# One decode step of attention plus feed-forward: half a weight tile on eight of the sixteen DMA engines

## The chip, the cores and the metric

The kernel runs on one core of a Trainium2 chip. The core has five engines with a queue each (TensorE, which the profile calls PE; VectorE, DVE; ScalarE, ACT; GpSimd, POOL; SyncE, SP) and sixteen DMA engines that bring data from HBM into SBUF (128 partitions). Matrix products end in PSUM. The metric is the device time of one execution in microseconds (us), the median of several; lower is better.

## The reference

One token for each of two batch rows. With `xn = layernorm(x)` (D = 1024):

```python
q = xn @ wq                                  # 32 heads of 128
p = softmax(q @ k.T * 128**-0.5)             # 4 key/value heads, 32768 cached keys each
attn = (p @ v) @ wo
h = silu(xn @ w1)                            # F = 3584
out = x + attn + h @ w2
```

All of it is float32. The caches of keys and values and the four weight matrices are read once, 331 MB in all; the arithmetic on them is small, since only two tokens are computed.

## The kernel before

**Tiling and staging.** Three buffers of 128 x 16384 floats (8 MB each), `bufA`, `bufB` and `bufC`, take everything that is streamed. First `wq` and `w1` come in: the projections give the queries (`qall`) and `pre`, the input of silu, and from it `hT` (L213 to L217), which holds `h` transposed: row tile f of the 3584 hidden values (28 tiles of 128) as 128 partitions x 2 tokens, spread over 32 columns. Then a loop of eight turns, one for each key/value head and batch row, loads two halves of the keys and two halves of the values. The two output projections come last: `wo` (32 row tiles of 128 x 1024) in bufA and bufC, then `w2` (28 row tiles) in bufB (16 tiles) and in bufA (12 tiles).

**What sets the order.** The order is written out by hand; each engine runs its own instructions in program order and waits on semaphores. SP issues all loads in one queue (`load`, L204 to L208), each after the TensorE work that frees its buffer. A load of 128 partitions is split over all sixteen DMA engines, and its semaphore has risen by 16 when all of them are done.

**The tail.** The last 12 row tiles of `w2` come in nine pieces (`stream`, L334 to L341, called at L378), cut smaller towards the end: 6 tiles, 2 tiles, 1, 1, 1, and the last tile in quarters. TensorE (`tiles`, L351) waits for the piece that holds a row tile (L353) and multiplies it. Row tiles are numbered through `wo` and `w2`: t = 0 to 31 is wo, 32 to 59 is w2. Up to t = 55 a tile is two matmuls of 512 columns, which go to two of the four 32-column strips of the array (`acc2`). From t = 56 on, a tile is four matmuls of 256 columns, j = 0 to 3, one for each strip of `acc` (L371). Ahead of t = 58 four `fold` matmuls add what `acc2` holds, which DVE has summed with x into `ob` (L363). The last tile, t = 59, is four groups of four matmuls of 64 columns, a group for each quarter. ACT then copies `acc` to SBUF and issues the store of the output (L388, L389).

The instructions of interest have helper lines in the profile: L98 is every matmul, L208 every load of SP after the first three, L52 a semaphore that the instruction stream counts down.

## Time and profile before

| | us |
|---|---|
| median of 3 runs | 774.31 |
| lowest and highest | 773.94 and 774.92 |
| the profiled execution, its own time | 773.65 |
| its span, first to last instruction | 772.2 |
| TensorE busy | 386.6 (50%) |
| VectorE busy | 120.7 (16%) |
| ScalarE busy | 27.3 (4%) |
| DMA, mean over the span | 429 GB/s |

The span is what the trace covers; some 1.5 us of the execution's own time lie around it. The profiled execution was a little shorter than the three runs. A share of DMA is the mean over the sixteen DMA engines, so 0.50 may be eight engines that are busy and eight that have nothing left. "Idle before" is the time that an engine stood still ahead of a group, with what ended it.

### The profile page before, as it was taken

How to read it: one execution, taken by the hardware profiler on the slowest of the kernel's cores; microseconds unless marked ns; L12 is line 12 of the kernel's file. 1: busy time of each engine (PE TensorE's matmuls, PEld its weight loads, DVE VectorE, ACT ScalarE, POOL GpSimd, SP SyncE). 2: the span in 40 equal slices, each digit the busy share in tenths (PEclk: the TensorE clock that was granted, in tenths of full speed). 3: DMA queues.
4: the chain of work that ended last, by engine and by line, in shares of the span. 5: the costliest groups of instructions: out<-in, count | busy, mean ns of one | idle time of the engine just before them, and what ended most of it. 6: DMA issues, size and time to landing. Idle time of an engine off the chain costs nothing. (4 is left out here: it accounts for less than half of the span.)

```text
span 772.2 us, 5903 instructions
## 1 busy us (share of the span) xinstructions
PE 386.6 (50%) x2736; PEld 122.7 (16%) x2736; DVE 120.7 (16%) x153; ACT 27.3 (4%) x33; POOL 3.0 (0%) x10
## 2 busy tenths in 40 slices
PE   1545645554545444645454545444645454545466
PEld 1111211111111111211111111111211111111112
DVE  2000013111311131113111311131113111311000
ACT  0000101000100010001000000010001000000000
POOL 1000000000000000000000000000000000000000
PEclk9977677677677677677677677677677677677679
DMA  9999999999999999999999999999999999999997
GB/s 384 435 435 435 431 435 435 435 435 435 435 435 435 435 435 431 431 435 435 435 431 431 435 435 435 435 435 435 435 435 435 435 431 435 435 435 435 421 417 321
DMA packets 7091, 331.48 MB, mean 429 GB/s; under 512 B 798, under 2 KB 1318, under 8 KB 1708
## 3 DMA queue, kind: packets, MB, share of 16 engines
q1 hardware_dynamic: 7056, 331.35, 99.4%
q8 instruction: 6, 0.10, 0.0%
q10 hardware_dynamic: 28, 0.02, 0.0%
q14 instruction: 1, 0.01, 0.0%
HBM read 331.37 MB, written 0.01 MB: 429 GB/s over the span
## 5 line engine op out<-in xcount | busy, mean ns | idle before, releaser
L98 PE MATMUL ps<-bufB,qT 128*32 128x512 f32 x512 | 72.7, 731 | 83.2 <-PEq L52 83.2
L98 PE MATMUL po<-bufB,st 128*32 128x512 f32 x512 | 71.5, 721 | 82.7 <-PEq L52 82.7
L98 PE MATMUL ps<-bufA,qT 128*32 128x512 f32 x512 | 71.7, 723 | 53.1 <-PEq L52 53.1
L98 PE MATMUL po<-bufA,st 128*32 128x512 f32 x512 | 72.2, 727 | 39.3 <-PEq L52 39.3
L276 DVE TENSOR_REDUCE ls<-st 128x8 f32<-128x1024 f32 x16 | 31.8, 1984 | 229.6 <-PE po L98 229.6
L251 DVE STREAM_TRANSPOSE st<-ps 128x1024 f32<-128x1024 f32 x16 | 20.0, 1250 | 250.6 <-PE ps L98 250.6
L98 PEld LDWEIGHTS ps<-bufB,qT 128*32 128x32 f32 x512 | 20.0, 131 | 136.0 <-issue 136.0
L98 PEld LDWEIGHTS po<-bufB,st 128*32 128x32 f32 x512 | 19.7, 130 | 134.5 <-issue 134.5
L98 PEld LDWEIGHTS ps<-bufA,qT 128*32 128x32 f32 x512 | 19.8, 130 | 98.4 <-issue 98.4
L98 PEld LDWEIGHTS po<-bufA,st 128*32 128x32 f32 x512 | 19.9, 131 | 85.0 <-issue 85.0
L253 DVE TENSOR_REDUCE mx<-st 128x8 f32<-128x1024 f32 x16 | 31.7, 1981 | 0.6
L273 ACT ACTIVATE st<-st 128x1024 f32<-128x1024 f32 x16 | 16.9, 1056 | 358.7 <-DVE st L272 358.0
L98 PE MATMUL ps<-bufB,xnT 128*32 128x512 f32 x112 | 18.3, 730 | 14.8 <-PEq L52 14.8
L272 DVE TENSOR_TENSOR st<-st,gmax 128x1024 f32<-128x1024 f32 x16 | 18.9, 1222 | 0.3
L98 PE MATMUL smA<-ident,rm 128*8 128x128 f32 x16 | 3.7, 317 | 29.5 <-PEq L52 29.5
L98 PE MATMUL ps<-bufC,xnT 128*32 128x512 f32 x64 | 8.6, 698 | 10.8 <-DMA bufC<-in_w 10.8
L98 PE MATMUL ps<-bufC,oT 128*32 128x512 f32 x64 | 8.5, 692 | 9.7 <-DMA bufC<-in_wo 9.7
L281 ACT COPY ob<-po 128x512 f32<-128x512 f32 x8 | 4.7, 585 | 236.7 <-PE po L98 236.7
L98 PE MATMUL smA<-lsum,ones 128*128 128x8 f32 x16 | 3.3, 278 | 19.2 <-PEq L52 19.2
L98 PE MATMUL ps<-bufA,oT 128*32 128x512 f32 x64 | 9.6, 766 | 6.6 <-DMA bufA<-in_wo 6.6
L98 PE MATMUL ps<-bufA,xnT 128*32 128x512 f32 x64 | 9.7, 773 | 5.0 <-PEq L52 5.0
L98 PE MATMUL ps<-bufB,hT 128*32 128x512 f32 x64 | 8.9, 702 | 4.8 <-DMA bufB<-in_w 4.8
(65 smaller groups left out, 102.1 us busy)
## 6 DMA issues: line engine op xcount, KB each, us to landing
bufB<-in_w SPq DMA_DIRECT2D x1, 6144.0 KB, 26.2
bufB<-in_w SPq DMA_DIRECT2D x1, 5632.0 KB, 42.7
bufA<-in_w SPq DMA_DIRECT2D x1, 3072.0 KB, 36.3
bufB<-in_w SPq DMA_DIRECT2D x1, 2560.0 KB, 48.5
bufA<-in_w SPq DMA_DIRECT2D x3, 512.0 KB, 40.0
bufA<-in_w SPq DMA_DIRECT2D x1, 1024.0 KB, 38.4
bufA<-in_w SPq DMA_DIRECT2D x4, 128.0 KB, 38.0
bufA<-in_kt SPq DMA_DIRECT2D x8, 29.3
```

Source lines behind the costliest of these rows:

```text
L98: return nc.tensor.matmul(o, lhsT, rhs, start=start, stop=stop)
L251: t = dve.mark(V.transpose(st[:, 2 * c:2 * c + 2].rearrange("p a j m -> p (a j m)"), pair[c]))
L253: m = V.tensor_reduce(mx[:, c, :], st[:, 2 * c:2 * c + 2].rearrange("p a j (r m) -> p m (a j r)", r=4), AX.X, ALU.max)
L272: act.wait(dve.mark(V.tensor_sub(e8[c], e8[c], gmax.to_broadcast([P, 128, REP]))))
L273: nc.scalar.activation(e8[c], e8[c], AF.Exp, scale=SCALE).then_inc(te, 1)
L276: m = V.tensor_reduce(ls[:, c, :], e8[c].rearrange("p n m -> p m n"), AX.X, ALU.add)
L281: nc.scalar.copy(ob, po).then_inc(tob, 1)
```

## The change

It concerns row tile 25 of `w2` (`LOW = FT - 3`, t = 57), the third last. Before, it came as one piece of 128 partitions x 1024 columns. Now its columns 0 to 511 come as a piece of 128 partitions x 512 columns. Its columns 512 to 1023, all 128 rows, go to partitions 0 to 63 of an unused part of bufA: rows 0 to 63 lie in the first 512 columns there, rows 64 to 127 behind them. One transfer with a semaphore of its own (`low`) does that, with the source's outermost dimension of size 8, each index covering eight neighbouring partitions.

Since rows 64 to 127 now stand on partitions 0 to 63, the values of `h` that they meet must stand there too. So one further matmul transposes them to partitions 0 to 63, a copy puts them into an added 29th column of `pre`, and silu runs over 29 columns instead of 28. In the output projection strips j = 2 and j = 3 of t = 57 take two matmuls each over 64 partitions, instead of one over 128. That tile waits for `low` and its own piece.

```diff
-    oT, hT = sb("oT", P, HQ, 32), sb("hT", P, FT, 32)
-    pre, sig, rsig = (sb(n, P, FT, B) for n in ("pre", "sig", "rsig"))
+    oT, hT = sb("oT", P, HQ, 32), sb("hT", P, FT + 1, 32)
+    pre, sig, rsig = (sb(n, P, FT + 1, B) for n in ("pre", "sig", "rsig"))
...
+        if u == 3:
+            j, i = divmod(LOW - 16, 4)
+            xo = ps[2 + u % 2][:, 8 * parts:8 * parts + B]
+            m = mm(xo, pr[u % 2][:n, i * P + 64:i * P + 192], ident[:n, 32 * j:32 * j + B])
...
+            if u == 3:
+                m = V.tensor_copy(pre[:, FT, :], xo)
...
+            if t == HQ + LOW:
+                pe.wait((low, 16))
...
                 for j in range(4):
+                    if t == HQ + LOW and j >= 2:
+                        for n in range(2):
+                            at2 = lowA + n * 512 + (j - 2) * QW
+                            m = mm(acc[32 * j:32 * j + 32, :], hT[:64, FT if n else LOW, :], bufA[:64, at2:at2 + QW],
+                                   False, False)
+                        continue
                     m = mm(acc[32 * j:32 * j + 32, :], lhsT, w[:, j * QW:(j + 1) * QW], t == PAIRED, False)
...
-    ends = [*stream(bufA, w2[:, W:], (0, 6 * D, 8 * D, 9 * D, 10 * D, lo, lo + QW, lo + 2 * QW, lo + 3 * QW,
-                                      lo + D), i_wo0)]
+    lowA, low = 12 * D, sem("low")
+    ends = [*stream(bufA, w2[:, W:], (0, 6 * D, 8 * D, 9 * D, 9 * D + D // 2), i_wo0)]
+    load(bufA[:64, lowA:lowA + D].rearrange("p (s n) -> p s n", s=2),
+         w2[:, LOW * D + D // 2:(LOW + 1) * D].rearrange("(s e r) n -> e r s n", s=2, e=8), low)
+    ends += [(10 * D, ends.pop()[1])]
+    ends += [*stream(bufA, w2[:, W:], (10 * D, lo, lo + QW, lo + 2 * QW, lo + 3 * QW, lo + D))]
```

On SP's queue the end of the program is, before, from the last load of values on (`in_w` is `w1` or `w2`, here `w2`; the size is partitions x columns):

```order
L208 DMA bufB<-in_v 128x16384 [waits pe]
L208 DMA bufA<-in_wo 128x16384 [waits pe]
L208 DMA bufC<-in_wo 128x16384
L208 DMA bufB<-in_w 128x11264 [waits pe]
L208 DMA bufB<-in_w 128x5120 [waits pe]
L208 DMA bufA<-in_w 128x6144 [waits pe]
L208 DMA bufA<-in_w 128x2048 [waits pe]
L208 DMA bufA<-in_w 128x1024 [waits pe] x3
L208 DMA bufA<-in_w 128x256 [waits pe] x4
```

and now, from the first load into bufA of `w2` on:

```order
L216 DMA bufA<-in_w 128x6144 [waits pe]
L216 DMA bufA<-in_w 128x2048 [waits pe]
L216 DMA bufA<-in_w 128x1024 [waits pe]
L216 DMA bufA<-in_w 128x512 [waits pe]
L216 DMA bufA<-in_w 64x2x512
L216 DMA bufA<-in_w 128x1024
L216 DMA bufA<-in_w 128x256 x4
```

One of the three pieces of one row tile has become a half piece and the new transfer right behind it; nothing else has moved.

On TensorE the same end is, before, from row tile 56 on (`piece6` to `piece12` are the pieces' semaphores, `dve` VectorE's sum in `ob`; the size is that of a matmul's output):

```order
L98 MATMUL acc<-bufA,hT 32x256 [waits piece6]
L98 MATMUL acc<-bufA,hT 32x256 x3
L98 MATMUL acc<-bufA,hT 32x256 [waits piece7]
L98 MATMUL acc<-bufA,hT 32x256 x3
L98 MATMUL acc<-ob,fold 32x256 [waits dve,piece8]
L98 MATMUL acc<-ob,fold 32x256 x3
L98 MATMUL acc<-bufA,hT 32x256 x4
L98 MATMUL acc<-bufA,hT 32x64 [waits piece9]
L98 MATMUL acc<-bufA,hT 32x64 x3
```

and now:

```order
L100 MATMUL acc<-bufA,hT 32x256 [waits piece6]
L100 MATMUL acc<-bufA,hT 32x256 x3
L100 MATMUL acc<-bufA,hT 32x256 [waits low,piece7]
L100 MATMUL acc<-bufA,hT 32x256 x5
L100 MATMUL acc<-ob,fold 32x256 [waits dve,piece8]
L100 MATMUL acc<-ob,fold 32x256 x3
L100 MATMUL acc<-bufA,hT 32x256 x4
L100 MATMUL acc<-bufA,hT 32x64 [waits piece9]
L100 MATMUL acc<-bufA,hT 32x64 x3
```

Row tile 57 has six matmuls instead of four and one more wait; the rest stands as it did.

## Rows read from the trace of the kernel before

**Rows 1.** The page: span, DMA by slices, DMA queues.

```profile
span 772.2 us, 5903 instructions
...
DMA  9999999999999999999999999999999999999997
...
q1 hardware_dynamic: 7056, 331.35, 99.4%
q8 instruction: 6, 0.10, 0.0%
```

**Rows 2.** The chain that ended last, in time: start, us, what.

```profile
685.76 29.96 DMA bufA<-in_wo
...
727.30 40.85 DMA bufA<-in_w
768.16 0.04 issue
768.20 1.65 PE acc L98 x48
769.85 0.02 issue
769.87 0.37 ACT ot L388
```

**Rows 3.** Windows: length, busy of each engine, TensorE clock, DMA share, GB/s.

```profile
764.00:765.20 1.20, 1.20 (x9) 0.22 (x5) 0.00 (x0) 0.00 (x0) 0.00 (x0) 0.50 1.03 410
767.00:767.40 0.40, 0.40 (x12) 0.26 (x8) 0.16 (x1) 0.00 (x0) 0.00 (x0) 1.00 1.02 356
767.40:767.60 0.20, 0.20 (x8) 0.13 (x4) 0.20 (x1) 0.00 (x0) 0.00 (x0) 1.00 0.81 272
...
767.80:768.20 0.40, 0.24 (x8) 0.00 (x1) 0.14 (x1) 0.00 (x0) 0.00 (x0) 1.00 0.51 179
768.20:768.80 0.60, 0.60 (x12) 0.42 (x16) 0.00 (x0) 0.00 (x0) 0.00 (x0) 1.00 0.40 138
768.80:769.00 0.20, 0.20 (x12) 0.13 (x4) 0.00 (x0) 0.00 (x0) 0.00 (x0) 1.00 0.24 82
769.00:769.20 0.20, 0.20 (x16) 0.11 (x9) 0.00 (x0) 0.00 (x0) 0.00 (x0) 1.00 0.01 0
```

**Rows 4.** Timeline of the tail: start, us, instructions, idle before.

```profile
766.99 1.05 PE L98 MATMUL acc<-bufA,hT 128*32 128x256 f32 x16
...
767.24 0.69 DVE L363 TENSOR_TENSOR ob<-ps,xres 128x512 f32<-128x512 f32 x1 [57.69 <-PE ps L98]
...
768.20 0.64 PE L98 MATMUL acc<-ob,fold 128*32 128x256 f32 x8 [0.16 <-DMA bufA<-in_w]
...
768.66 1.15 PE L98 MATMUL acc<-bufA,hT 128*32 128x256 f32 x40
```

**Rows 5.** TensorE's groups by shape from 750 us on: busy, mean ns.

```profile
L98 PE MATMUL acc<-bufA,hT 128*32 128x256 f32 x24 | 1.7, 379 | 0.0
```

**Rows 6.** SP's own issues at the end: start, us, count.

```profile
725.51 20.33 SPq L208 DMA_DIRECT2D bufA<-in_w  x9
```

**Rows 7.** Windows in mid stream, columns as in Rows 3.

```profile
300.00:320.00 20.00, 9.61 (x64) 2.60 (x64) 2.07 (x2) 0.58 (x1) 0.00 (x0) 0.74 1.02 442
```

**Rows 8.** By shape, 84 to 97 us: busy, mean ns, idle before.

```profile
L98 PE MATMUL ps<-bufA,qT 128*32 128x512 f32 x4 | 1.1, 1052 | 7.8 <-PEq L52 7.8
...
L98 PE MATMUL ps<-ident,pr 96*128 96x6 f32 x8 | 1.0, 254 | 0.0
...
L194 DVE COPY pre<-ps 128x24 f32<-128x24 f32 x1 | 0.2, 183 | 0.7 <-PE ps L98 0.7
```

**Rows 9.** GpSimd at the start of the program: start, us.

```profile
2.72 0.84 POOL L111 MEMSET hT<- 128x896 f32 x1
```

## The prediction

> **What bounds the kernel now.** I read the page first [rows 1]. The DMA engines are full in all of the 40 slices but the last, and the one queue that brings in 331 MB takes 99.4% of sixteen engines' span. So the kernel is a stream of bytes with something at each end, and only two kinds of change can move it: fewer engine-microseconds in the stream, or a shorter end. This change moves the same bytes, so only the end is left. Next comes the chain of waits [rows 2]: before 768.16 us it is loads alone; then 1.65 us of TensorE, 0.37 us of ScalarE's copy, and the store. What is to be seen there is that the last wait on a load ends at 768.2, and everything behind it is short.

> Third, the DMA shares in narrow windows at the end [rows 3]. Up to 767.4 all sixteen engines work (1.02). Then the share falls in steps: 0.81, 0.51, 0.40, 0.24, and 0.01 after 769.0. A share of 0.40 is 0.40 x 16 = 6.4 engines. So the sixteen don't end together: some nine or ten run out between 767.4 and 768.2, and six or seven go on until 769.0. The page has six packets of instructions on another queue, 0.10 MB or about 16 KB each [rows 1]. Six engines that each carried one of them would be late in just this way. I take that as likely. The rows don't say which six they are.

> Fourth, TensorE in the same stretch [rows 4]. Its last group ends at 768.66 + 1.15 = 769.81, 0.8 us after the stream. Ahead of it TensorE has been busy with one gap of 0.16 us before the fold matmuls at 768.20. So TensorE is hardly ahead of the loads: both arrive at the end together. That decides how I cost the change.

> **The bytes.** The half tile is 128 x 512 x 4 B = 256 KB. Before, the whole piece put 32 KB on each engine, in rows of 4 KB. Rate of an engine with such rows: 410 GB/s at a share of 1.03, over 16, is 24.9 GB/s [rows 3]; so 1.32 us. With rows of 1 KB, in the last quarters, it is 138 / 0.40 / 16 = 21.6 GB/s. Rows of 2 KB, which both new transfers have, are not in the trace; I take the middle, 23.2, with these two as bounds. If the transfer uses engines 0 to 7, they carry 16 + 32 = 48 KB: 2.12 us, 0.80 more than before (0.66 to 0.96). Engines 8 to 15 carry 16 KB: 0.71 us, 0.61 less (0.56 to 0.66).

> What that is worth depends on where the six late engines are. If all are in the upper eight, they end at 769.0 - 0.6 = 768.4, and the lower eight, all early ones, at 767.4 to 768.2 plus 0.8, 768.2 to 769.0. The stream ends at 768.4 to 769.0: nothing to 0.6 us earlier. If some are in the lower eight, it ends 0.8 later. I hold the first for likelier, by a guess of about two to one: six packets that follow one another in one queue may well have gone to neighbouring engines, but which ones no row says.

> **TensorE at the end.** Two matmuls of 256 columns are added to row tile 57. A matmul leaves two records, so the 16 records of tiles 56 and 57 are four rounds of four: (1.05 - 0.38) / 3 = 0.22 us a round, with 0.38 from the mean of that group [rows 4, 5]. A tile is two rounds, 0.44, because its four strips work side by side. Tile 57 starts at 766.99 + 0.44 = 767.43 and has issued at 767.87; the fold starts at 768.20. That leaves 0.33 of cover. Now strips 2 and 3 each take two matmuls one after the other. If the strips run independently, the tile is 0.44 longer, and 0.11 stands out of the cover. If matmuls issue strictly in order, strip 3 cannot start before the second matmul of strip 2 has, and the tile is 0.88 longer: 0.55 stands out. No row shows two matmuls in a row on one strip. The rounds, in which records start in order, are nearest to the second; since the fold of strips 0 to 2 can start beside the last of them, I take 0.45. All that follows on TensorE is later by that: fold, tile 58, the last tile, ScalarE's copy, the store.

> Can an earlier stream give it back? Hardly. The fold also waits for VectorE's sum, which ends at 767.24 + 0.69 = 767.93 [rows 4]. So at most 768.20 - 767.94 = 0.26 is to be had on the side of the loads, and the longer tile 57 has used it up.

> **The added wait.** Tile 57 waits for `low`; behind it stand the fold, tile 58 and the last tile. On an engine that ends at 768.2, row tile 58 and the last tile, 64 KB an engine, take 2.6 to 3.0 us, so its old share of tile 57 ended at 765.2 to 765.6. With 0.8 more, and some 0.5 until the semaphore is seen (an estimate: TensorE ends 0.8 after the stream's last bytes, and that holds the last matmuls too), that is 766.5 to 766.9, ahead of 767.43: hidden. [...]

> **Edits that I cost at nothing.** SP issues one load more. Its nine issues stand between 725.51 and 745.84, over 20 us before the bytes are needed [rows 6]; without that cover it would be some 0.4 us. The added matmul and copy at 88 us are about 0.25 + 0.18 us [rows 8], silu's two columns more are a few ns on three instructions; behind them TensorE waits 7.8 us for the first keys, and VectorE's chain ends well before. Uncovered they would be 0.45 us. GpSimd clears 928 columns instead of 896 ahead of the load of x: 0.84 x 32 / 896 = 0.03 us [rows 9], behind which wq still streams.

> **The sum.** The profiled execution took 773.65. Plus 0.45 is 774.1. It lies 0.66 below the median of the runs shown, so on that median the forecast is 774.31 + 0.45 = 774.8, with 774.4 to 774.9 by the bounds 0.11 and 0.55.

> [...]

> [...]

> **The rivals.**
> A. Some late engines are among the lower eight. The stream ends 0.8 later and TensorE with it: 774.31 + 0.8 = 775.1 (774.97 to 775.27). For it: nothing in the trace tells the halves apart. Against: six of sixteen need not straddle.
> [...]
> [...]
> D. A gain: strips independent, late engines all in the upper eight, the fold as early as VectorE's sum allows: 0.11 - 0.26 = -0.15, 774.15.
> E. The transfer spreads over all sixteen engines after all. Then the shares at the end stay as they are, and only TensorE's 0.45 remains: 774.8.

> **How the numbers follow.** Forecast 0.42, A 0.17, B 0.20, C 0.12, D 0.05, E 0.04. A measurement of this kernel tells a change from none at about 0.2%, 1.55 us; the three runs alone lie 1 us apart. Only C, and the top of A and B with a stroke of bad luck, passes it upward: slower 0.13. Nothing in the rows gives 1.55 us back: faster 0.03, for what I have not seen. Same 0.84. The range of 8 in 10 goes from D less some of the runs' spread, 773.9, to C, 776.2.

> **What would show it.** The half rows are right if the share after 767.4 falls differently: by the forecast it stays high until about 768.2 and drops quickly, since both halves end closer together. [...] The TensorE term is right if 20 records of 256 columns ahead of the fold take about 1.5 us or more (1.05 + 0.44) and the fold follows without a gap. The forecast is wrong if TensorE waits for a load in the last microsecond, or if the clock, 0.50 up to 765.2 [rows 3], falls elsewhere and stretches the same matmuls.

## The result: 1.8 us slower, and the profile after

The changed kernel takes 776.12 us, the median of 11 runs (775.34 to 776.71), against 774.31 for the kernel before, also 11 runs (773.89 to 775.02). The ratio is 1.0022, with an interval of 1.0014 to 1.003: slower by 1.8 us, between 1.1 and 2.3. The forecast was 774.8. The time lies inside the range of 773.9 to 776.2, by 0.1 us, near its upper end, which stood for rival C. That is luck: it came about in another way.

The page of the kernel after: span, then all DMA packets with the small ones counted; last, the same count before.

```profile
span 774.7 us, 5918 instructions
...
DMA packets 7236, 331.50 MB, mean 428 GB/s; under 512 B 814, under 2 KB 1334, under 8 KB 1852
```
```profile
DMA packets 7091, 331.48 MB, mean 429 GB/s; under 512 B 798, under 2 KB 1318, under 8 KB 1708
```

The span was 772.2 [rows 1], so this execution (776.19 us) is 2.5 longer than the profiled one of before (773.65); the medians are 1.8 apart. The loads move the same bytes. Of packets under 512 B there were 798 before; now there are 16 more, for one load more. The landing events in the trace have the same number: the semaphore of every load into bufA for `w2` rises sixteen times, before and after, and `low` does so from 765.94 to 769.04 us. I read this as sixteen engines, not eight; the records name no engine.

The chain of waits of the kernel after: start, us, what.

```profile
726.75 0.43 SPq L216
727.18 0.04 issue
727.23 41.81 DMA bufA<-in_w
769.04 0.14 issue
769.18 3.11 PE acc L100 x60
772.28 0.02 issue
772.31 0.37 ACT ot L410
```

Before, loads held the chain until 768.16, and 48 records of TensorE followed [rows 2]. Now a load holds it until 769.04, and 60 records follow, in 3.11 us instead of 1.65. The load is the same in name, but TensorE waits for it earlier in its program: ahead of row tile 57, not ahead of the fold.

The timeline of TensorE in the kernel after: start, us, group, idle time before it and what ended it.

```profile
767.02 0.60 PE L100 MATMUL acc<-bufA,hT 128*32 128x256 f32 x8
769.18 1.62 PE L100 MATMUL acc<-bufA,hT 128*32 128x256 f32 x12 [1.55 <-DMA bufA<-in_w]
770.72 0.64 PE L100 MATMUL acc<-ob,fold 128*32 128x256 f32 x8
771.18 1.06 PE L100 MATMUL acc<-bufA,hT 128*32 128x256 f32 x40
```

The 16 records of tiles 56 and 57, which ran in one piece [rows 4], are split. Tile 56 has its 8 at the old time, then TensorE waits 1.55 us, and tile 57 has its 12 from 769.18 to 770.72, where the fold starts. Behind the fold nothing has changed but the time of day: the end is 771.18 + 1.06 = 772.24, before 769.81.

Windows of the kernel after, the first three of them the same as in [rows 3]; columns as there, TensorE clock, DMA share and GB/s last.

```profile
764.00:765.20 1.20, 1.20 (x8) 0.20 (x4) 0.00 (x0) 0.00 (x0) 0.00 (x0) 0.50 1.12 268
767.00:767.40 0.40, 0.40 (x12) 0.12 (x4) 0.13 (x1) 0.00 (x0) 0.00 (x0) 1.00 1.16 202
768.20:768.80 0.60, 0.00 (x0) 0.00 (x0) 0.00 (x0) 0.00 (x0) 0.00 (x0) 1.00 0.99 263
...
769.00:770.00 1.00, 0.82 (x8) 0.35 (x10) 0.00 (x0) 0.00 (x0) 0.00 (x0) 1.00 0.68 235
...
770.40:770.80 0.40, 0.40 (x8) 0.08 (x8) 0.00 (x0) 0.00 (x0) 0.00 (x0) 1.00 0.30 102
770.80:771.20 0.40, 0.40 (x12) 0.23 (x15) 0.00 (x0) 0.00 (x0) 0.00 (x0) 1.00 0.03 10
```

Read share and GB/s together. From 764.0 to 765.2 the engines are as full as before (1.12 against 1.03), but move 268 GB/s instead of 410; from 767.0 to 767.4 it is 202 instead of 356. So all engines are at work, and each packet takes longer. The packet records of the trace (start, duration and size of each DMA packet) show it directly: the 4 KB packets, which belong to row tiles 56 and 58 and not to the new load, take up to 0.49 us, where in t3 (below) none takes more than 0.17. The bytes that are late by then are caught up at the end: at 768.2 to 768.8 the share is still 0.99, before it was 0.40, and it falls to nothing at about 770.9, before at 769.0.

The sum of this profile against that of before: tile 57 starts 1.75 us later (769.18 against 767.43); it takes 1.54 instead of 0.44, 1.10 more; 0.33 of cover ahead of the fold is used up. 1.75 + 1.10 - 0.33 = 2.52, and the fold is at 770.72 instead of 768.20. The rest of the difference of the spans, -0.02, is rounding and the last matmuls.

The edits that the prediction hid are hidden. Timeline around 89 us of the kernel after, the added copy and the next wait of TensorE; then SP's issues at the end.

```profile
89.16 0.15 DVE L203 COPY pre<-ps 128x2 f32<-128x2 f32 x1
...
96.76 1.08 PE L100 MATMUL ps<-bufA,qT 128*32 128x512 f32 x4 [7.74 <-PEq L53]
...
725.43 35.27 SPq L216 DMA_DIRECT2D bufA<-in_w  x10
```

TensorE still waits 7.74 us for the first keys (7.8 in [rows 8]). SP's issues now last until 760.7, 15 us longer than in [rows 6]; experiment t3 has ten issues and the same length, at no cost.

### The profile page after: what moved, and what is told of

The parts are those of the page before. It is cut to its first block, busy times and chain, and to the rows that moved or that the text cites. A ratio compares the mean times of both kernels' runs of the same rounds, so it can differ in the third digit from the quotient of the medians.

```text
span 774.7 us, 5918 instructions
## 1 busy us (share of the span) xinstructions
PE 388.9 (50%) x2742; PEld 123.7 (16%) x2742; DVE 120.8 (16%) x154; ACT 27.3 (4%) x33; POOL 3.0 (0%) x10
## 5 line engine op out<-in xcount | busy, mean ns | idle before, releaser
L280 DVE TENSOR_TENSOR st<-st,gmax 128x1024 f32<-128x1024 f32 x16 | 18.9, 1221 | 0.3
L100 PE MATMUL smA<-ident,rm 128*8 128x128 f32 x16 | 3.7, 317 | 29.4 <-PEq L53 29.4
```

Of the source, the lines that this page charges most:

```text
L100: return nc.tensor.matmul(o, lhsT, rhs, start=start, stop=stop)
L280: act.wait(dve.mark(V.tensor_sub(e8[c], e8[c], gmax.to_broadcast([P, 128, REP]))))
```

## The experiments

The theory after the result: sixteen engines carry the new load; into 64 partitions it takes longer than its bytes ask, so it lengthens the stream; and the 64-row matmuls cost more than reckoned. The expectations set two theories side by side. By the bytes theory a load costs its bytes over the engines that carry it. By the lanes theory it also matters which partitions are written at the same moment: a load into 64 runs at half the rate of one into 128, and of two with the same bytes on eight engines, such as m3 and m4, one can cost twice the other. m1 to m4 measure both: 187 GB/s against 442, and 40.1 us against 18.9. "Lanes" is my name for what engines would share then; no run shows them as such, only times and rates. An engine moves 27.1 GB/s in mid stream (442 / 1.02 / 16 [rows 7]). The rivals: the bytes on fewer engines alone, the wait alone, the matmuls alone, and one load more as such.

### What a load into 64 partitions costs in mid stream: m1 to m4

Four kernels add a load of 4.19 MB to the kernel before, into a buffer that is idle at that moment, far from both ends: it is issued at about 358 us, and its packets run from about 384 us on. Its shape differs, and m4 makes two loads of it. (m1 reads 128 rows of `w1` of half the length, the others 64 rows.) (`extra` is a semaphore of its own, waited for ahead of the tail.)

```diff
     if it == 3:
# m1_128: 128 partitions
+        load(bufC[:, :8192], w1[:, :8192], extra, last_of[2])
# m2_64: 64 partitions, sixteen engines
+        load(bufC[:64, :], w1[:64, :W], extra, last_of[2])
# m3_eight: eight engines, eight neighbouring partitions each
+        load(bufC[:64, :], w1[:64, :W].rearrange("(r e) n -> e r n", e=8), extra, last_of[2])
# m4_eight_lanes: eight engines, four neighbouring partitions each, twice
+        for g in range(2):
+            load(bufC[32 * g:32 * g + 32, :], w1[32 * g:32 * g + 32, :W].rearrange("(r e) n -> e r n", e=8),
+                 extra, last_of[2])
```

> The kernel before with one load more in mid stream: 4 MB (128 partitions x 32 KB) into bufC, which lies unused there. Bytes theory (a load costs its bytes over the engines that carry it) and lanes theory (a load also costs its bytes over the write lanes that its partitions reach) agree: 4.19 MB / 433 GB/s = 9.7 us more, 784 us.

> The same 4 MB as 64 partitions (0 to 63) x 64 KB, rows in plain order. Number of engines: if it is split over 16 engines, 16 tiny packets more than in before stand in the page, if over 8, 8. Bytes theory with 16 engines: 9.7 us more, 784. Lanes theory (64 partitions reach half of the lanes, 8 x 27.1 GB/s): 19.3 us more, 793.6. Bytes theory with 8 engines would also give 19.3, so the count of tiny packets decides what is meant.

> The same 4 MB to partitions 0 to 63, with the source's rows taken in an order (r e), e = 8 outermost, that cannot be merged into one run of 64 rows: eight engines with eight neighbouring partitions each (8 tiny packets more). Bytes theory: 512 KB an engine / 27.1 GB/s = 19.3 us more, 793.6. [...]

> The same 4 MB to partitions 0 to 63 by two loads of 32 partitions, each on eight engines with four neighbouring partitions, so that engine e serves partitions 4e to 4e+3 and 32+4e to 32+4e+3 (16 tiny packets more, 8 a load). Both theories: 19.3 us more, 793.6, since no two engines meet in a lane. Beside m3_eight it tells lanes from bytes.

| added load | time | more than before (774.66) | ratio, interval |
|---|---|---|---|
| m1_128 | 784.56 | 9.9 | 1.013 (1.0101 to 1.0159) |
| m2_64 | 797.29 | 22.6 | 1.0295 (1.0255 to 1.0334) |
| m3_eight | 814.76 | 40.1 | 1.052 (1.049 to 1.0551) |
| m4_eight_lanes | 793.6 | 18.9 | 1.0247 (1.0217 to 1.0277) |

Each has two runs (m2: 796.13 and 798.46), before has three. One window of each, 385 to 405 us, in the order m1, m2, m3, m4.

```profile
385.00:405.00 20.00, 11.54 (x74) 4.76 (x74) 2.62 (x5) 0.59 (x1) 0.00 (x0) 0.67 1.02 442
```
```profile
385.00:405.00 20.00, 11.86 (x74) 4.78 (x74) 2.62 (x5) 0.59 (x1) 0.00 (x0) 0.67 0.91 187
```
```profile
385.00:405.00 20.00, 10.49 (x74) 3.74 (x74) 2.62 (x5) 0.59 (x1) 0.00 (x0) 0.76 0.96 203
```
```profile
385.00:405.00 20.00, 10.32 (x74) 3.70 (x74) 2.62 (x5) 0.58 (x1) 0.00 (x0) 0.76 0.97 419
```

All four keep the engines full (0.91 to 1.02). m1 and m4 move 442 and 419 GB/s, m2 and m3 187 and 203. m3 and m4 bring the same rows of `w1` on eight engines each; they differ in which partitions are written at the same time, and in one load against two. With four neighbours each, twice, the rate is double that with eight, 419 GB/s against 203, and the cost half: 18.9 us against 40.1 for the same bytes on eight engines. So the price is one of which partitions are written together, not of bytes per engine. On sixteen engines it is 187 GB/s into 64 partitions against 442 into 128.

One thing goes beyond it. In m3 only eight engines carry the load. Had the other eight gone on at the 27.1 GB/s of mid stream, they alone would have moved 217 GB/s; the row has 203 for all sixteen, at a share of 0.96. So the engines without a part in the load were slowed too. The packet records agree: 120 packets of 64 KB took over 4 us (2.42 is usual), and the load has only 64. The lanes theory doesn't say why.

How many engines a load used I read from the small packets, in the pages of m2 and of m3.

```profile
DMA packets 7171, 335.68 MB, mean 422 GB/s; under 512 B 814, under 2 KB 1334, under 8 KB 1724
```
```profile
DMA packets 7163, 335.68 MB, mean 413 GB/s; under 512 B 806, under 2 KB 1326, under 8 KB 1716
```

m2 has 16 more than 798, m3 has 8 more. The landings of `extra` are as many, 8 in m3. In m3 the outermost index `e` steps by one row and `r` by eight, so the two can't be one run; this load shows 8. In the changed kernel the source is `(s e r) n -> e r s n`: `e` steps by eight rows and `r` by one, which together is a plain run of 64 rows. The built program's load is 64 x 2 x 512, and it shows 16.

One thing is left over. Reckoned from the 9.9 us of m1, m2 (half the rate) and m4 (half the engines) should cost twice as much, and m3 (both) four times. m3 (40.1 for 39.6) and m4 (18.9 for 19.8) come out as reckoned. m2 is 22.6 for 19.8; two runs don't settle that (19.8 is the lower end of its interval), but its packets do: between 300 and 500 us those of 64 KB took 12.6 us an engine more than at their usual 2.42, and half rate for the load's 64 alone would be 9.7.

### One part of the change alone: t1, t2, t3

t1 has the matmuls of the change and the loads of before. It leaves out the upper half of those rows, multiplying the lower 64 twice.

```diff
-            if t == HQ + LOW:
-                pe.wait((low, 16))
...
-                            at2 = lowA + n * 512 + (j - 2) * QW
+                            at2 = lowA + (j - 2) * QW
...
-    lowA, low = 12 * D, sem("low")
...
+    lowA = 9 * D + D // 2
+    ends = [*stream(bufA, w2[:, W:], (0, 6 * D, 8 * D, 9 * D, 10 * D, lo, lo + QW, lo + 2 * QW, lo + 3 * QW,
+                                      lo + D), i_wo0)]
```

> The changed kernel's arithmetic with the loads of before: row tile 57 comes as one piece of 128 partitions, no transfer low. Strips 2 and 3 still take two matmuls over 64 partitions each, both on rows 0 to 63, so rows 64 to 127 of the tile are left out for columns 512 to 1023. My sum put 0.45 us on the matmuls (0.11 to 0.55): 774.8. If the loads alone make the change (lanes theory), 774.3 to 774.5.

t2 has the loads of the change and leaves out the second matmul of strips 2 and 3.

```diff
-                        for n in range(2):
+                        for n in range(1):
```

> The loads of the changed kernel, with its waits and its 29th column of silu, but one matmul for each of strips 2 and 3 of row tile 57 (rows 64 to 127 of columns 512 to 1023 left out). Lanes theory: the end is that of the changed kernel less the length of the two matmuls, 775.5 to 776.0, with TensorE idle 1.5 us ahead of row tile 57. If the matmuls were the cause: 774.3.

t3 is the kernel before with the half tile as a load of its own, over all 128 partitions.

```diff
-    ends = [*stream(bufA, w2[:, W:], (0, 6 * D, 8 * D, 9 * D, 10 * D, ...
+    ends = [*stream(bufA, w2[:, W:], (0, 6 * D, 8 * D, 9 * D, 9 * D + D // 2, 10 * D, ...
```

> The kernel before with row tile 57 in two pieces of 128 partitions x 512 columns, both of 2 KB rows, all arithmetic as before. Lanes theory: a second half on 128 partitions reaches all lanes, so only the smaller rows and one load more count: 0.05 to 0.2, 774.4. If it is the cut into smaller rows that costs: near 776.

Beside the kernel before at 774.33 (27 runs) they took: t1 774.52, ratio 1.0011 (1.0002 to 1.002); t2 775.62, 1.0016 (1.0007 to 1.0025); t3 774.24, 0.9996 (0.9987 to 1.0006). One load more costs nothing, and nor do rows of 2 KB. The load into half the partitions, with four matmuls two of which are on 64 rows, costs 1.3 us. The matmuls alone cost 0.2 by the medians, 0.85 by the ratio, which the scatter of 1.6 us among the 11 runs of t1 doesn't settle. Both have matmuls on 64 rows, so the two can't simply be added to the 1.8 of the change; no run has the load without them.

TensorE's timeline at the end of t1, then of t2.

```profile
762.04 4.93 PE L100 MATMUL ps<-bufA,hT 128*32 128x512 f32 x32 [3.46 <-DMA bufA<-in_w]
766.79 2.02 PE L100 MATMUL acc<-bufA,hT 128*32 128x256 f32 x20
768.75 0.64 PE L100 MATMUL acc<-ob,fold 128*32 128x256 f32 x8
769.20 1.06 PE L100 MATMUL acc<-bufA,hT 128*32 128x256 f32 x40
```
```profile
769.00 1.18 PE L100 MATMUL acc<-bufA,hT 128*32 128x256 f32 x8 [1.28 <-DMA bufA<-in_w]
770.11 0.64 PE L100 MATMUL acc<-ob,fold 128*32 128x256 f32 x8
770.56 1.15 PE L100 MATMUL acc<-bufA,hT 128*32 128x256 f32 x40
```

In t1 the 20 records run without a gap; less 0.44 for tile 56, tile 57 has 768.75 - 766.79 - 0.44 = 1.52 us. The fold is 0.55 later than in [rows 4]. In t2 tile 57 has no matmul more than before, four of them, and still takes 1.11 instead of 0.44, only because strips 2 and 3 use 64 rows. So 0.67 us comes from the 64 rows as such, and some 0.4 from the two matmuls added. t2 also waits 1.28 us for the load: tile 57 starts at 769.00, 1.57 later than before, and TensorE ends at 771.71, 1.9 later. So the load, with its wait, does most of the damage. (The profile of t2 is of its slowest run, 776.35, 0.7 above its median.)

### Eight engines after all, with eight and with four partitions each: t4, t5

With the rows of this half tile laid out in another order in memory, the load can be split in eight as the change intended. t4 has eight neighbouring partitions an engine, as m3 (40.1 us), and t5 four, as m4 (18.9).

```diff
# t4_eight
+    for s in range(2):
+        load(bufA[:64, lowA + 512 * s:lowA + 512 * (s + 1)],
+             w2[64 * s:64 * s + 64, LOW * D + D // 2:(LOW + 1) * D].rearrange("(r e) n -> e r n", e=8), lows[s])
# t5_eight_lanes
+    for i in range(4):
+        s, h = divmod(i, 2)
+        load(bufA[32 * h:32 * h + 32, lowA + 512 * s:lowA + 512 * (s + 1)],
+             w2[64 * s + 32 * h:64 * s + 32 * h + 32, LOW * D + D // 2:(LOW + 1) * D].rearrange("(r e) n -> e r n", e=8),
+             lows[i])
```

> The changed kernel with its half tile truly on eight engines, eight neighbouring partitions each: two loads of 64 partitions x 512 columns with the source's rows in an order that does not merge into one run (the rows are laid out for it beforehand); arithmetic as in the changed kernel. [...] Bytes theory: 0.8 on the stream, 775.1 to 775.6.

> The same half tile on eight engines by four loads of 32 partitions, each engine with four neighbouring partitions, so that no two engines share a lane. Both theories: 0.8 us of bytes on the late engines of the lower eight and row tile 57's longer matmuls behind them: 775.1 to 775.6. Were all late engines in the upper eight, 774.5 to 774.8.

Beside before at 774.02 (30 runs), t4 took 776.2, ratio 1.0027 (1.0016 to 1.0037); t5 took 775.05, 1.0012 (1.0003 to 1.0021). Their loads did run on eight engines: in the trace each of these loads has eight landing events. So the change as it was meant would have been about as slow as the change as it is, and four partitions an engine instead of eight take back half of that. TensorE's timeline and two windows of t4:

```profile
770.04 1.62 PE L100 MATMUL acc<-bufA,hT 128*32 128x256 f32 x12 [2.31 <-DMA bufA<-in_w]
771.59 0.64 PE L100 MATMUL acc<-ob,fold 128*32 128x256 f32 x8
```
```profile
771.20:771.60 0.40, 0.40 (x8) 0.01 (x2) 0.00 (x0) 0.00 (x0) 0.00 (x0) 1.00 0.07 23
771.60:772.00 0.40, 0.40 (x10) 0.28 (x12) 0.00 (x0) 0.00 (x0) 0.00 (x0) 1.00 0.04 13
```

Tile 57 waits 2.31 us, and one engine (0.07 x 16 = 1.1) still loads at 771.6. (This profile too is of the slowest run, 777.33, 1.1 above the median.) The same two views of t5:

```profile
762.05 6.43 PE L100 MATMUL ps<-bufA,hT 128*32 128x512 f32 x32 [3.67 <-DMA bufA<-in_w]
768.31 2.02 PE L100 MATMUL acc<-bufA,hT 128*32 128x256 f32 x20
770.26 0.64 PE L100 MATMUL acc<-ob,fold 128*32 128x256 f32 x8
```
```profile
764.00:766.00 2.00, 2.00 (x12) 0.40 (x8) 0.00 (x0) 0.00 (x0) 0.00 (x0) 0.50 1.07 404
766.00:768.00 2.00, 2.00 (x16) 0.52 (x12) 0.00 (x0) 0.00 (x0) 0.00 (x0) 0.57 0.92 335
...
768.80:769.00 0.20, 0.20 (x8) 0.05 (x2) 0.20 (x1) 0.00 (x0) 0.00 (x0) 1.00 0.09 31
769.20:769.60 0.40, 0.40 (x6) 0.24 (x6) 0.05 (x1) 0.00 (x0) 0.00 (x0) 1.00 0.07 26
```

The stream is back at 404 GB/s, most engines end by 768.8, and TensorE waits for no load at the end; one engine (0.07 x 16) goes on until 769.6. What bounds this execution is TensorE: its 32 records of the piece before take 6.43 us instead of 4.93 in t1, with the granted clock at 0.50 from 764 to 766 and 0.57 until 768, so the lower of the two levels, 0.50 and 1.00, that the traces of before and after show. In [rows 3] it was full again by 767.0. The profile is of a run of 775.64, near the slowest of t5 (774.52 to 775.68), so its clock need not be that of the other runs, and the median stands.

### Where TensorE's time goes, and an earlier load: t7, t8, t6

t7 is t5 with the matmuls of tile 57 in another order, strips 2, 3, 2, 3 and not 2, 2, 3, 3, and a finer cut of the piece of six tiles. t8 is the kernel before with that cut alone.

```diff
# t7_lanes_order
+                if t == HQ + LOW:
+                    order = [(0, None), (1, None), (2, 0), (3, 0), (2, 1), (3, 1)]
# t7_lanes_order and t8_cut
-    (0, 6 * D, 8 * D, 9 * D, ...
+    (0, 3 * D, 6 * D, 8 * D, 9 * D, ...
```

> t5_eight_lanes with the six matmuls of row tile 57 in the order strip 0, 1, 2, 3, 2, 3, and the piece of six row tiles cut into two of three, so that TensorE starts earlier. In-order theory of the matmuls: tile 57 takes 0.88 us instead of about 1.5; stream as in t5_eight_lanes. 774.7 to 775.2. If the order of the matmuls doesn't matter, as t5_eight_lanes.

> The kernel before, with nothing changed but the piece of six row tiles cut into two of three. TensorE's chain from that piece on has one gap of 0.16 us only, so loads and matmuls bound the end together; with the earlier start of TensorE the loads alone do: 0 to 0.3 us less, 774.0 to 774.3.

t7 took 774.76, ratio 1.0011 (1.0002 to 1.002); t8 773.94, 0.9997 (0.9988 to 1.0006), no difference from before (774.02). TensorE's timeline of t7, then of t8:

```profile
767.63 1.61 PE L100 MATMUL acc<-bufA,hT 128*32 128x256 f32 x12 [1.09 <-DMA bufA<-in_w]
769.17 0.64 PE L100 MATMUL acc<-ob,fold 128*32 128x256 f32 x8
769.62 1.06 PE L100 MATMUL acc<-bufA,hT 128*32 128x256 f32 x40
```
```profile
767.40 0.64 PE L98 MATMUL acc<-bufA,hT 128*32 128x256 f32 x8 [0.63 <-DMA bufA<-in_w]
768.69 0.64 PE L98 MATMUL acc<-ob,fold 128*32 128x256 f32 x8 [0.65 <-DMA bufA<-in_w]
```

The order made no difference: tile 57 takes 1.54 us as in the changed kernel. The time of t7 lies in the range of the in-order theory, 774.7 to 775.2, but its reason doesn't hold. That the matmuls issue in order was my reason for the bound of 0.88, and this is not it. What fits t2, t7 and the changed kernel alike is that strips of 128 rows and strips of 64 rows don't run side by side: 0.44 for strips 0 and 1; then 0.44 for each pair of 64-row matmuls on strips 2 and 3; and some 0.1 at each of the two changes. That gives 0.44 + 0.44 + 0.2 = 1.08 for t2 (1.11 measured) and 1.52 with the second pair (1.54). The single records show it. Before, the four strips of a tile start within 0.03 us of one another, and a round follows the last by 0.22. In t2 the 128-row strips start at 769.00 and again at 769.21 to 769.24; the 64-row strips start together at 769.55, 0.31 behind, and again at 769.79; the fold, on 128 rows, starts at 770.11, again 0.31 behind. In t8, with t7's cut and the old tile 57, the fold itself waits for a load until 768.69; t7 is there at 769.17, and its end 0.36 later. The medians are 0.8 apart.

t6 is the changed kernel with the new load issued ahead of the piece of six tiles, so that its bytes are there long before tile 57.

```diff
+    load(bufA[:64, lowA:lowA + D]..., low, i_wo0)
     ends = [*stream(bufA, w2[:, W:], (0, 6 * D, 8 * D, 9 * D, 9 * D + D // 2), i_wo0)]
-    load(bufA[:64, lowA:lowA + D]..., low)
```

> The changed kernel with the transfer low issued first of the loads into bufA, ahead of the piece of six row tiles, so that it lands long before row tile 57 needs it. Lanes theory: the transfer still takes about 0.65 us more of all engines than its bytes, wherever it stands, so 0.65 plus the matmuls' term, 775.0 to 775.4; the 1.5 us wait ahead of row tile 57 is gone. If the end of the stream only suffers from the wait at row tile 57: 774.6. If the cost is the same wherever it stands: 776.1.

It took 777.41 beside 774.33, ratio 1.0043 (1.0029 to 1.0056): 3.1 us more, where 0.7 to 1.1 were expected. Windows and TensorE's timeline of t6:

```profile
752.00:758.00 6.00, 6.00 (x52) 1.60 (x44) 0.00 (x0) 0.00 (x0) 0.00 (x0) 0.86 1.02 272
758.00:762.00 4.00, 0.55 (x6) 0.00 (x0) 0.00 (x0) 0.00 (x0) 0.00 (x0) 1.00 1.02 436
```
```profile
764.65 4.97 PE L100 MATMUL ps<-bufA,hT 128*32 128x512 f32 x32 [6.10 <-DMA bufA<-in_w]
769.45 2.02 PE L100 MATMUL acc<-bufA,hT 128*32 128x256 f32 x20
771.40 0.64 PE L100 MATMUL acc<-ob,fold 128*32 128x256 f32 x8
```

The wait ahead of tile 57 is gone, as intended. But for 6 us the full engines move 272 GB/s instead of 436: (436 - 272) x 6 us = 0.98 MB are late, 2.2 us at that rate. By its packet records from 740 us on, t6 took 29.4 engine-microseconds more than t3 did for packets of the same sizes, 1.84 us for each of the sixteen engines; the changed kernel took 30.3, or 1.90. The piece of six tiles lands later by that and by the load's own 256 KB, which now stand ahead of it, some 0.6 us at 410 GB/s. TensorE starts on it at 764.65 instead of 762.04 in t1, 2.6 later, and from there on it works without a gap to the end. So the price of this load belongs to the stream, wherever it stands; moving it ahead only moves what is late.

No version here is faster than the kernel before.

## Why the prediction was wrong on the mechanism and near on the number

**"The same bytes, so only the end is left."** The step left a third thing out: the stream can grow longer without a byte more, if packets take longer. It did, by 1.9 us at its end, which is what the longer packets add up to (1.90), and t6 shows the same price elsewhere (1.84). That the DMA engines are the bound held throughout.

**The transfer on engines 0 to 7.** It failed. The load ran on sixteen, by the 16 small packets and the 16 landings, so the terms +0.80 and -0.61 never came to pass. That it would use eight engines, and those numbered 0 to 7, was my assumption from the size 8 of the outermost index in the source text; no run shows the numbers. The counts here are 16 for a run of 64 rows and 8 where the outermost index can't be merged, and what I left out is the merged 64x2x512 that stands in the order of the changed kernel ahead of the prediction. So the title is wrong in its eight engines, too. The question of which engines are late fell away with it. t5 answers it for its own run: in each of its four eight-way loads seven landings lie within 1.0 us and the eighth 0.8 behind (766.59 against 765.75 in the first). So one late engine is among the eight that carried it (in m4 three of eight landed late), and the guess of two to one, that all late ones are outside the eight that carry the load, would have failed as well.

**Rivals B and E.** What came was sixteen engines (E, 0.04) and at once a load slower than its bytes, which is what B (0.20) stood for, there on eight engines. `low` landed late, at 769.04, and TensorE stood idle for 1.55 us ahead of tile 57. E was priced with the shares at the end unchanged, which missed that a load into 64 partitions is slower on sixteen engines as well (m2: 187 GB/s against 442 in m1). The 0.20 for B was low: in m3 the slowing came in full, 40.1 us for a reckoned 39.6.

**`low` hidden at 766.5 to 766.9.** It failed by more than 2 us: `low` landed at 769.04, TensorE waits 1.55 and starts tile 57 at 769.18. This is the greatest term of the result: 1.75 of the 2.52 between the two profiles.

**TensorE, 0.45 (0.11 to 0.55).** The place was right, the size was not: 1.10 - 0.33 = 0.77 in the profile of the change, 0.55 for the fold of t1. I assumed that 64-row matmuls overlap with 128-row ones as before. t2 shows that they don't (1.11 instead of 0.44 without any matmul more), and t7 that the order of the strips has no part in it. The 20 records with the fold behind them came as written, in t1 without a gap, in the changed kernel with the wait between tiles 56 and 57.

**The hidden edits.** Right in each: the early matmul and copy, SP's tenth issue (t3: 774.24 against 774.33), and the fold's second wait on VectorE.

**The number.** Forecast 774.8, measured 776.12. The range's upper end came from case C: late engines among eight (A) and a slowed load on those eight (B) at once, 1.8 us on the median. No run shows that term by itself; the runs showed a slowed stream on sixteen (1.90) and longer matmuls (0.77, or 0.55 in t1) in its place, and t4, truly on eight, 2.2 with its matmuls. That the two numbers meet is luck. The interval of 1.1 to 2.3 us lies on both sides of the prediction's bound of 1.55: that it is slower is clear, that it passes the bound is not. The chance of 0.13 for slower rested on C; a slowed load by itself was to pass the bound only "with a stroke of bad luck".

**What stays open.** At about 400 GB/s, 256 KB take 0.65 us, so half the rate should cost 0.65 more and the load costs 1.9. Where the rest falls can be read from the packet records. Of the 30.3 engine-microseconds that the packets of the change took more than those of t3, 9.9 are in packets of 2 KB, half of which are the new load's; 13.6 are in the 4 KB packets of tiles 56 and 58 and 6.2 in the 1 KB packets of the last tile. So two thirds of the price are paid by other loads' packets. They are slow from about 764 us until the new load has landed at 769.04, and take their usual time before and behind that. It isn't a matter of sixteen engines: t4, on eight engines with eight partitions each, has 21.3 in the same way (10.0 in packets of 4 KB), and t5, on eight with four each, has none (-0.5). What stays open is why other loads' packets are slowed, up to three times, and why in m3 even those on engines that carry nothing of the load are. No run takes that apart.

## What to carry to other kernels

In a kernel whose DMA engines are full, a load's shape is a cost like its bytes: before you narrow a load's partitions, allow for more than its bytes (4.19 MB cost 9.9 us into 128 partitions and 22.6 into 64), and look at GB/s beside the share, since a full share hides a halved rate (1.02 at 442 GB/s in m1, 0.96 at 203 in m3). Read a load's dimensions from the built program, not from the text that made it; equally spaced indices merged here, and the count was 16 for the merged 64x2x512, not the 8 of the source text. And a matmul on half the rows doesn't fit in beside its full neighbours for nothing: with two of its four on 64 rows, a tile of 0.44 us took 1.11 here.
